# A first weight row loaded from two queues, and another number of unused products around the output projection

## The chip, the cores and the metric

The kernel runs on one core of a Trainium2 chip. The metric is the device time of one execution in microseconds (us), the median of several runs. A core has five engines that run at the same time: TensorE (PE in the profile, with its weight loads as PEld), VectorE (DVE), ScalarE (ACT), GpSimd (POOL) and SyncE (SP). SyncE computes nothing here, it issues the transfers. 16 DMA engines carry the transfers between memory and the core's buffers; SyncE and ScalarE each have a queue of their own from which these engines are fed.

## The reference

One decoding step of a transformer block for two sequences: a layer norm, attention over the last 2048 positions of a cache of 8192 (32 heads of 192), an output projection, and a gated feed-forward part, each with its residual.

```python
q = (x @ wq).reshape(B, Sq, Hq, Dh)            # B = 2, Sq = 1, D = 640, Hq = 32, Dh = 192
scores = einsum("bhqd,bhkd->bhqk", q, k) * Dh ** -0.5    # k, v: the last W = 2048 rows of the caches
o = einsum("bhqk,bhkd->bhqd", softmax(scores), v)
A = o.reshape(B, Sq, Hq * Dh) @ wo
h = x + A(layernorm(x))
out = h + (gelu(layernorm(h) @ w_gate) * (layernorm(h) @ w_up)) @ w_down     # F = 1536
```

All inputs are bfloat16. The kernel reads the windows of both caches and all weights once; it multiplies each of them with only two rows of x, h or the heads' results.

## The kernel before, in words

**How the work is written.** Each engine's program is a list of operations. `P.op` notes what an operation reads and writes (the names in `R`, `W` and `X`) and derives the semaphore waits between the engines from it; within an engine the order is that of the calls. An operation with `dma=` is a transfer, and each such name has a semaphore of its own. The helpers `pe`, `dve`, `act` and `pool` add an operation to their engine.

**How the work is staged.** A ring of three slots of 49152 bytes a partition takes everything large in turn: wq, eight loads each of K and V (6144 KB apiece), wo in two pieces (36 and 12 of its 48 rows a partition), then four of w_gate's five rows a partition, w_up in two pieces and w_down in four. `load` puts a transfer into a list, and `pump` issues from the head of the list on SyncE, as soon as all that lay in its place has been read (`done`). K is transposed on TensorE (L555), copied back by DVE and ScalarE, multiplied with q (L613), and the softmax of four groups at a time goes with V through TensorE (L669). The groups run in a loop of four trips on PE and DVE.

**The start.** x (`xrow`) is issued by ScalarE (L435). The first row a partition of w_gate does not go into the ring but into a buffer of its own, `wgh` (`load_wg0`, L397 to L399), issued by SyncE ahead of wq; it is read only by the first of the gate products near the end (L832). Then follow wq and the first loads of K (L372, the one line of all ring loads). x is turned into columns by PE (L496), normalised, and the products with wq (L575) wait for that and for wq's landing.

**The end.** After the loop, `spread(0)`, `behind(14)`, `heads_done(1)` and `spread(1)` gather the heads' results of both sequences into `ot`. `oproj(0)` and `oproj(1)` multiply `ot` with wo's two pieces (L727: 72 and 24 products of 320 columns, on four column strips of TensorE at once), beginning with two products that add x (L722). Then come the second normalisation (L735 to L821), the gate products with w_gate (L832), their columns through TensorE and the gelu on DVE and ScalarE (L841 to L869), the products with w_up (L832 again, into `ops`), their columns and the product with the gelu (`uT`), the products with w_down's four pieces (L881; the last piece has four products), a copy of the result (`yrow`, L887) and the store (L888).

**Unused products.** `keep_busy(n, w)` issues n products of the identity matrix with constants (`cf`) into a PSUM bank, whose result nobody reads. In 32-bit floats a product of 512 columns is two matmul rows of the profile (L752). They are placed in the loop's sums, behind q, and four times around the end: one product behind `behind(14)`, two behind `spread(1)`, and two between `oproj(0)` and `oproj(1)`.

Of the kernel before, what the change touches and what calls it, by code (L numbers as in the profile page):

```python
# [14 lines left out]
NC5 = D // 128  # L15
# [232 lines left out]
def bass_sequential_preLN__sliding_block_cached__geglu_ffn__decode_kernel(  # L248
# [12 lines left out]
    with ExitStack() as ctx:  # L261

        def sb(name, shape, dt):
            return ctx.enter_context(nc.sbuf_tensor(name, shape, dt))
# [31 lines left out]
        wgh = sb("wgh", [128, 1, F], BF16)  # L296
# [54 lines left out]
        P = _Prog()  # L351
        looped = []

        where, live, queue, used = {}, [], [], set()
# [33 lines left out]
        def load_wq():  # L388
            load("wq", WQ_AT, 2 * NC5 * HQ * DH, A_wq.rearrange("(p c) n -> p c n", c=NC5),
                 lambda v: v.rearrange("p (c n) -> p c n", n=HQ * DH), "wq")  # L390
# [4 lines left out]
                 lambda v: v.rearrange("p (kk n) -> p kk n", n=D), f"wo{i}")  # L395

        def load_wg0():  # L397
            where["wg", 0] = wgh[:, :, :], ["wgh"]
            P.op("sp", lambda e: e.dma_start(wgh[:, 0, :], B_w_gate.rearrange("(p c) f -> p c f", c=NC5)[:, 0, :]), W=["wgh"], dma="wg0")  # L399

        def load_ffn():
            load(("wg", 1), WG_AT, 2 * (NC5 - 1) * F, B_w_gate.rearrange("(p c) f -> p c f", c=NC5)[:, 1:NC5, :],
# [17 lines left out]
        def pe(fn, R=(), W=(), X=(), cls=0):  # L420
            return P.op("pe", fn, R, W, X, cls=cls)
# [10 lines left out]
        def tt(out, a, b, op):  # L432
            return lambda e: e.tensor_tensor(out=out, in0=a, in1=b, op=op)  # L433

        P.op("act", lambda e: e.dma_start(xrow[0:2, :], A_x[:, 0, :]), W=["xrow"], dma="dx")  # L435
        load_wg0()
        load_wq()
        for i in range(2 * NQ):
            load_k(i)
# [267 lines left out]
        def spread(b):  # L707
            pe(lambda e: e.matmul(sps[:, 0:DH], lhsT=colsel[:, :], rhs=onrm[:, b, :], start=True, stop=True), R=["colsel", ("onrm", b)], X=["s"])
            dve(tt(sm[:, 0:DH].rearrange("p (c k) -> p c k", c=4), sps[:, 0:DH].rearrange("p (c k) -> p c k", c=4),
                   oht[:, :].unsqueeze(2).to_broadcast([128, 4, 48]), ALU.mult), R=["oht"], W=["sm"], X=["s"])  # L710
            dve(lambda e: e.tensor_reduce(out=ot32[:, :], in_=sm[:, 0:DH].rearrange("p (c k) -> p k c", c=4), axis=AX.X, op=ALU.add),
                R=["sm"], W=["ot32"])
            dve(lambda e: e.tensor_copy(ot[:, :, b], ot32[:, :]), R=["ot32"], W=["ot"])

        def oproj(i):
            wo, wtoks = where["wo", i]
            k0, k1 = WOC[i]

            def fn(e):
                if i == 0:  # L720
                    for h in range(2):
                        e.matmul(m1[32 * h:32 * h + 2, 192:512], lhsT=identb[0:2, 0:2], rhs=xrow[0:2, 320 * h:320 * (h + 1)],  # L722
                                 start=True, stop=False, tile_position=(0, 32 * h), skip_group_check=True)
                for kk in range(k0, k1):
                    for h in range(2):
                        r = 2 * (kk % 2) + h
                        ins = e.matmul(m1[32 * r:32 * r + 2, 192:512], lhsT=ot[:, kk, :],  # L727
                                       rhs=wo[:, kk - k0, 320 * h:320 * (h + 1)], start=(kk == 1),
                                       stop=(kk >= 46), tile_position=(0, 32 * r), skip_group_check=True)
                return ins  # L730

            pe(fn, R=wtoks + ["ot", "xrow", "identb"], X=["m1"])
            done(("wo", i))
            if i == len(WOC) - 1:
                dve(lambda e: e.tensor_tensor_reduce(out=hrow[0:98, :], in0=m1[0:98, 192:512], in1=hrow[0:98, :], scale=1.0, scalar=0.0,  # L735
                                                     op0=ALU.add, op1=ALU.add, accum_out=rs[0:98, :]), R=["hrow"], W=["hrow", "rs"], X=["m1"])
# [12 lines left out]
        def keep_busy(n, w=4):  # L749
            def fn(e):  # L750
                for k in range(n):
                    ins = e.matmul(tps[3][:, 0:128 * w], lhsT=identf[:, :], rhs=cf[:, 0:w, :].rearrange("p k x -> p (k x)"), start=True, stop=True)  # L752
                return ins

            pe(fn, R=["identf", "cf0", "cfm"], X=[("t", 3)])
# [39 lines left out]
        keep_busy(1)  # L795
        heads_done(1)
        spread(1)
        keep_busy(2)
        for i in range(len(WOC)):
            oproj(i)  # L800
            if i == 0:
                keep_busy(2)

        pe(lambda e: e.matmul(tps[3][:, 0:2], lhsT=rs[0:98, :].to_broadcast([98, 128]), rhs=bsel[0:98, :], start=True, stop=True),
           R=["rs", "bsel"], X=[("t", 3)])
# [47 lines left out]
        def rjb(t):  # L853
# [18 lines left out]
            W=[("osb", 0), ("osb", 1)], X=["o"])  # L872
        vT = ffn_columns(urow, [("osb", 0), ("osb", 1)], tps[1], 1)
        dve(tt(uT[:, :, 0:17:16].rearrange("p (r j) b -> p r j b", r=4), vT, rjb(ga[:, 0, :]), ALU.mult), R=["ga0"], W=["uT"], X=[("t", 1)])
        for i, (f0, f1) in enumerate(WDC):
            wd, wtoks = where["wd", i]

            def fn(e, f0=f0, f1=f1, wd=wd):
# [10 lines left out]
             dma="dout")  # L889
# [43 lines left out]
```

## Time and profile before

| what | us |
|---|---|
| median of 3 runs | 291.8 (291.45 to 292.17) |
| the profiled execution | 291.8 |
| its span, first to last instruction | 290.5 |
| PE busy in the span | 192.6 (66%) |
| DVE busy | 144.2 (50%) |
| ACT busy | 94.8 (33%) |
| POOL busy | 17.4 (6%) |
| HBM read | 122.29 MB, 421 GB/s over the span |

The profile is one execution. Its page gives the busy time of each engine, the span in 40 slices, the DMA queues, the chain of work that ended last, the costliest groups of instructions and the DMA issues. A row of a group or of the timeline has the start and the duration in us, the engine, the line of the kernel, the operation, what it writes and reads, the shape and the number of instructions; in brackets stands the idle time of the engine ahead of it, with what ended it. In a table of stretches, each row has its bounds, its length, the busy time (and the instructions) of PE, PEld, DVE, ACT and POOL, the TensorE clock that was granted (1.00 is full speed), the mean share of the 16 DMA engines that was busy, and the GB/s that they moved. A DMA row gives the size of one issue and the time from its issue to its landing. Span and time differ by what lies around the first and the last instruction.

### The profile page before, as it was taken

The numbers are of one execution on the slowest core, as the hardware profiler recorded it, in microseconds if no ns is written. First come the engines' busy times: TensorE is split into PE (matmuls) and PEld (weight loads), VectorE is DVE, ScalarE is ACT, GpSimd is POOL, SyncE is SP. The second block draws the span as 40 slices with busy tenths as digits, with TensorE's granted clock in tenths as the row PEclk, the third lists the DMA queues.
The fourth block names the chain that finished last, engine by engine and source line by source line (L and its number), as shares of the span: only waits on it lengthen the run. The fifth ranks groups of instructions, "written<-read, shape, count | busy, mean of one in ns | idle before, by whom it ended". The sixth has DMA issues, their size and how long they took to land.

```text
span 290.5 us, 6244 instructions
## 1 busy us (share of the span) xinstructions
PE 192.6 (66%) x2587; PEld 149.2 (51%) x2587; DVE 144.2 (50%) x379; ACT 94.8 (33%) x128; POOL 17.4 (6%) x44
## 2 busy tenths in 40 slices
PE   1007378865962788688607886886078868879785
PEld 1004276654830677477206774772067747726443
DVE  6100036781474067757720777577206775776022
ACT  1001026652430067356100673561006735610001
POOL 7500200000020000000200000002000000000000
PEclk9999959999797599999975999999759999999785
DMA  8999999999999999999999999999999999999994
GB/s 325 415 492 440 423 435 433 429 433 429 433 429 433 433 433 433 428 433 433 433 433 433 433 433 433 433 433 433 433 433 433 433 433 433 423 419 395 412 413 160
DMA packets 3915, 122.45 MB, mean 422 GB/s; under 512 B 446, under 2 KB 576, under 8 KB 1216
## 3 DMA queue, kind: packets, MB, share of 16 engines
q1 hardware_dynamic: 3900, 122.29, 97.9%
q8 instruction: 8, 0.13, 0.2%
q14 instruction: 3, 0.02, 0.0%
q10 hardware_dynamic: 4, 0.00, 0.0%
HBM read 122.29 MB, written 0.00 MB: 421 GB/s over the span
## 4 chain that ended last, share of the span: by engine, by line
DMA 44%; PE 35%; issue 10%; DVE 8%; ACT 3%; SPq 0%; DVEq 0%
DMA ring<-in_A_v_cache_dram 24%; PE tpp L555 18%; DMA ring<-in_A_k_cache_dram 13%; DMA ring<-in_A_wo_dram 8%; PE ops L669 5%; PE m L669 4%; DVE eblk L657 2%; PE sps L613 2%; DVE ktr L566 2%; DVE et L653 2%; PE m L727 2%; ACT ktr L564 1%; ACT eexp L628 1%; PE tpp L752 1%; PE m L881 1%
## 5 line engine op out<-in xcount | busy, mean ns | idle before, releaser
L555 PE MATMUL tpp<-identf,ring 128*128 128x128 f32 x768 | 94.6, 283 | 19.3 <-DVE ktr L566 11.6
L564 ACT ACTIVATE ktr<-tpp 128x1024 bf16<-128x1024 bf16 x80 | 76.7, 1019 | 85.9 <-PE tpp L555 85.9
L555 PEld LDWEIGHTS tpp<-identf,ring 128*128 128x128 f32 x768 | 86.8, 145 | 28.0 <-DVE ktr L566 12.5
L566 DVE COPY ktr<-tpp 128x1024 bf16<-128x1024 bf16 x112 | 76.0, 690 | 39.9 <-PE tpp L555 38.2
L613 PE MATMUL sps<-ktr,rq 128*32 128x512 bf16 x384 | 24.8, 387 | 14.1 <-DVE ktr L566 14.1
L669 PE MATMUL ops<-ring,eblk 128*32 128x192 bf16 x512 | 15.9, 290 | 24.2 <-DMA ring<-in_A_v_cache_dram 24.2
L669 PEld LDWEIGHTS ops<-ring,eblk 128*32 128x32 bf16 x512 | 14.2, 121 | 25.5 <-DMA ring<-in_A_v_cache_dram 24.7
L628 ACT ACTIVATE eexp<-sm,nms 128x512 bf16<-128x512 f32 x16 | 11.6, 722 | 41.0 <-DVE nms L624 41.0
L613 PEld LDWEIGHTS sps<-ktr,rq 128*32 128x32 bf16 x384 | 9.9, 94 | 24.5 <-ACT ktr L564 17.8
L752 PE MATMUL tpp<-cf,identf 128*128 128x512 f32 (+1 forms) x62 | 22.5, 504 | 0.0
L657 DVE COPY eblk<-et 32x512 bf16<-32x512 bf16 x64 | 18.5, 289 | 1.8
L624 DVE CUSTOM_DVE_ANT_1 sm<-sps,mska 128x512 f32<-128x512 f32 x16 | 11.0, 687 | 16.4 <-issue 16.2
L433 POOL TENSOR_TENSOR rq<-qs,mask 128x192 bf16<-128x192 bf16 x16 | 7.8, 518 | 178.5 <-PE sps L613 162.0
L669 PE MATMUL m<-ring,eblk 128*32 128x192 bf16 x512 | 14.8, 275 | 2.8 <-issue 2.8
L669 PEld LDWEIGHTS m<-ring,eblk 128*32 128x32 bf16 x512 | 13.7, 119 | 3.0 <-issue 3.0
L575 PE MATMUL tpp<-ring,xnT 128*32 128x384 bf16 x80 | 5.1, 430 | 14.9 <-DMA ring<-in_A_wq_dram 14.9
L700 DVE SCALAR_TENSOR_TENSOR osum<-ops,wp,osum 128x192 f32<-128x192 f32 x4 | 1.7, 418 | 26.5 <-PE ops L669 26.4
L752 PEld LDWEIGHTS tpp<-cf,identf 128*128 128x128 f32 x62 | 10.0, 195 | 7.4 <-issue 7.3
L653 DVE STREAM_TRANSPOSE et<-eexp 128x512 bf16<-128x512 bf16 x16 | 11.3, 706 | 1.0
L575 PEld LDWEIGHTS tpp<-ring,xnT 128*32 128x32 bf16 x80 | 2.9, 125 | 16.7 <-issue 15.0
L598 DVE CAST qs<-ops 128x384 bf16<-128x384 f32 x1 | 0.6, 559 | 19.9 <-PE ops L593 19.9
L582 ACT ACTIVATE qrow<-tpp 128x768 bf16<-128x768 f32 x1 | 0.8, 811 | 19.4 <-PE tpp L575 19.4
(138 smaller groups left out, 84.8 us busy)
## 6 DMA issues: line engine op xcount, KB each, us to landing
ring<-in_A_k_cache_dram SPq DMA_DIRECT2D x8, 6144.0 KB, 29.0
ring<-in_A_v_cache_dram SPq DMA_DIRECT2D x8, 6144.0 KB, 24.1
ring<-in_A_wq_dram SPq DMA_DIRECT2D x1, 7680.0 KB, 21.1
ring<-in_A_wo_dram SPq DMA_DIRECT2D x1, 5760.0 KB, 22.5
ring<-in_A_wo_dram SPq DMA_DIRECT2D x1, 1920.0 KB, 21.5
ring<-in_B_w_gate_dram SPq DMA_DIRECT2D x1, 1536.0 KB, 24.8
ring<-in_B_w_up_dram SPq DMA_DIRECT2D x1, 1536.0 KB, 28.0
ring<-in_B_w_down_dram SPq DMA_DIRECT2D x1, 960.0 KB, 20.2
```

The lines of the kernel that those rows point to most:

```text
L433: return lambda e: e.tensor_tensor(out=out, in0=a, in1=b, op=op)
L555: ins = e.transpose(bank[:, 128 * u:128 * (u + 1)], kv[:, off:off + 128], identf[:, :])
L564: act(lambda e, dst=dst, src=src: e.activation(out=dst, in_=src, func=ACT.Copy), W=[("kt", n)], X=[x])
L566: dve(lambda e, dst=dst, src=src: e.tensor_copy(dst, src), W=[("kt", n)], X=[x], cls=0)
L575: ins = e.matmul(tps[0][32 * r:32 * (r + 1), 0:384], lhsT=xnT[:, c, 32 * J:32 * (J + 1)], rhs=wq[:, c, 1536 * J + 384 * r:1536 * J + 384 * ...
L613: ins = e.matmul(sps[32 * hg:32 * (hg + 1), :], lhsT=rq[:, k, hg, :], rhs=cols, start=(k == 0), stop=(k == 5), tile_position=(0, 32 * hg))
L624: dve(lambda e: e.tensor_tensor_reduce(out=sm[:, :].rearrange("p (u x) -> p u x", x=32), in0=sps[:, :].rearrange("p (u x) -> p u x", x=32) ...
L628: act(lambda e: e.activation(out=eexp[:, :], in_=sm[:, :], func=ACT.Exp, bias=nms[:, n:n + 1], scale=-1.0, accum_out=zr[:, n:n + 1]), R=[( ...
L653: dve(lambda e: e.transpose(et[:, :], eexp[:, :]), R=["eexp"] + [("eb", 0, 3)] * (g % 2), W=["et"], cls=0)
L657: dve(lambda e, hg=hg: e.tensor_copy(eblk[32 * hg:32 * (hg + 1), g % 2, :, hg, :], et[32 * hg:32 * (hg + 1), :].rearrange("p (a x) -> p a ...
L669: ins = e.matmul(bank[32 * r:32 * (r + 1), 0:DH], lhsT=eblk[:, g % 2, a, :, :].rearrange("p s x -> p (s x)")[:, r:128:4], rhs=vv[:, DH * t ...
L752: ins = e.matmul(tps[3][:, 0:128 * w], lhsT=identf[:, :], rhs=cf[:, 0:w, :].rearrange("p k x -> p (k x)"), start=True, stop=True)
```

## The change

The first row of w_gate is cut into two halves of 64 partitions. SyncE issues the lower one and ScalarE the upper one; each half has a semaphore and a token of its own, and the gate products wait for both. ScalarE issues its half ahead of x instead of x first. Behind `spread(1)` there are four unused products instead of two, and between `oproj(0)` and `oproj(1)` one instead of two.

```diff
         def load_wg0():
-            where["wg", 0] = wgh[:, :, :], ["wgh"]
-            P.op("sp", lambda e: e.dma_start(wgh[:, 0, :], B_w_gate.rearrange("(p c) f -> p c f", c=NC5)[:, 0, :]), W=["wgh"], dma="wg0")
+            where["wg", 0] = wgh[:, :, :], [("wgh", 0), ("wgh", 1)]
+            src = B_w_gate.rearrange("(p c) f -> p c f", c=NC5)
+            for k, eng in enumerate(("sp", "act")):
+                P.op(eng, lambda e, k=k: e.dma_start(wgh[64 * k:64 * (k + 1), 0, :], src[64 * k:64 * (k + 1), 0, :]), W=[("wgh", k)], dma=f"wg0{k}")
...
+        load_wg0()
         P.op("act", lambda e: e.dma_start(xrow[0:2, :], A_x[:, 0, :]), W=["xrow"], dma="dx")
-        load_wg0()
         load_wq()
...
         spread(1)
-        keep_busy(2)
+        keep_busy(4)
         for i in range(len(WOC)):
             oproj(i)
             if i == 0:
-                keep_busy(2)
+                keep_busy(1)
```

## The prediction

> **What bounds the kernel now.** I read the page first: the span, its slices and the DMA queues. The second line below is what the DMA engines moved in 40 slices of 7.26 us.
>
> ```profile
> span 290.5 us, 6244 instructions
> ...
> GB/s 325 415 492 440 423 435 433 429 433 429 433 429 433 433 433 433 428 433 433 433 433 433 433 433 433 433 433 433 433 433 433 433 433 433 423 419 395 412 413 160
> ...
> q1 hardware_dynamic: 3900, 122.29, 97.9%
> q8 instruction: 8, 0.13, 0.2%
> ```
>
> The 16 DMA engines move 433 GB/s in most slices, and little less in the others from the third to the last but one, and SyncE's queue alone fills 97.9% of their time. So the stream of loads is the bound: the end can come forward only if the stream starts sooner or if less is left to do after its last piece. I therefore went to both ends of the span, first the end. The DMA issues with their time to landing, and then SyncE's part of the timeline, give the moment at which each late weight is there (issue start plus landing time):
>
> ```profile
> ring<-in_A_wq_dram SPq DMA_DIRECT2D x1, 7680.0 KB, 21.1
> ring<-in_A_wo_dram SPq DMA_DIRECT2D x1, 5760.0 KB, 22.5
> ring<-in_A_wo_dram SPq DMA_DIRECT2D x1, 1920.0 KB, 21.5
> ring<-in_B_w_gate_dram SPq DMA_DIRECT2D x1, 1536.0 KB, 24.8
> ring<-in_B_w_up_dram SPq DMA_DIRECT2D x1, 1536.0 KB, 28.0
> ...
> wgh<-in_B_w_gate_dram SPq DMA_DIRECT2D x1, 384.0 KB, 3.3
> ring<-in_B_w_up_dram SPq DMA_DIRECT2D x1, 384.0 KB, 28.5
> ...
> ring<-in_B_w_down_dram SPq DMA_DIRECT2D x1, 160.0 KB, 21.3
> ```
> ```profile
> 247.59 0.34 SPq L372 DMA_DIRECT2D ring<-in_A_wo_dram  x1
> 253.08 0.33 SPq L372 DMA_DIRECT2D ring<-in_A_wo_dram  x1
> 253.46 0.43 SPq L372 DMA_DIRECT2D ring<-in_B_w_gate_dram  x1
> 253.94 0.91 SPq L372 DMA_DIRECT2D ring<-in_B_w_up_dram  x2
> ...
> 266.36 0.94 SPq L372 DMA_DIRECT2D ring<-in_B_w_down_dram  x1
> ```
>
> wo's first piece lands at 247.59 + 22.5 = 270.09, its second at 253.08 + 21.5 = 274.58, w_gate's four rows at 253.46 + 24.8 = 278.26, w_up's first piece at 253.94 + 28.0 = 281.94, its second at 282.92 (its issue starts 0.43, the time of the issue before it, ahead of 253.94 + 0.91 = 254.85, so at 254.42). The last piece of w_down lands at 266.36 + 21.3 = **287.66**. Now the timeline of the last 25 us, cut to the rows of the chain that ended last:
>
> ```profile
> 266.37 1.88 PE L752 MATMUL tpp<-cf,identf 128*128 128x512 f32 x4
> ...
> 270.19 0.30 PE L722 MATMUL m<-xrow,identb 2*2 2x320 bf16 x2 [1.93 <-DMA ring<-in_A_wo_dram]
> ...
> 270.41 3.98 PE L727 MATMUL m<-ring,ot 128*2 128x320 bf16 x72
> ...
> 274.32 2.25 PE L752 MATMUL tpp<-cf,identf 128*128 128x512 f32 x4
> ...
> 276.50 0.99 PE L727 MATMUL m<-ring,ot 128*2 128x320 bf16 x24
> ...
> 280.19 0.39 PE L832 MATMUL sps<-ring,hnT 128*2 128x384 bf16 x4
> ...
> 283.01 1.77 PE L832 MATMUL ops<-ring,hnT 128*2 128x384 bf16 x20
> ...
> 286.54 1.78 PE L881 MATMUL m<-ring,uT 128*17 128x160 bf16 x48 [0.32 <-DVE uT L433]
> 288.37 0.32 DVE L887 CAST yrow<-m 113x160 bf16<-113x160 f32 x1 [1.89 <-PE m L881]
> ```
>
> PE starts the first half of the output projection 0.10 after its load has landed (270.19 against 270.09), so I take 0.10 as the step from landing to PE. PE then has 1.93 us of idle time behind it. The clock, by stretches (the figure behind the five engines, then the DMA share and GB/s), shows what that does:
>
> ```profile
> 266.00:270.00 4.00, 2.25 (x7) 0.94 (x6) 1.03 (x3) 0.00 (x0) 0.00 (x0) 1.00 0.79 328
> ...
> 271.00:272.00 1.00, 1.00 (x28) 0.62 (x24) 0.00 (x0) 0.00 (x0) 0.00 (x0) 0.74 0.90 381
> ...
> 274.00:275.00 1.00, 1.00 (x9) 0.50 (x2) 0.00 (x0) 0.00 (x0) 0.00 (x0) 0.55 1.01 418
> ...
> 282.00:283.00 1.00, 0.68 (x3) 0.46 (x3) 0.27 (x1) 0.00 (x0) 0.00 (x0) 0.50 0.99 407
> ```
>
> A stretch at 0.74 is half of it at 1.00 and half at 0.50, one at 0.55 a tenth of it at 1.00: the granted clock falls to 0.50 at about 271.5 and comes back near 274.9; the 72 products of wo's first piece, and part of the unused products behind them, run at half speed. Near 282 it falls again for the rest.
>
> **The change, part by part.** *Four unused products instead of two behind the last spread.* One `keep_busy` product is two rows of the profile: the four rows at 266.37 take 1.88, 0.47 each. Eight rows take 3.76 and end at 270.13, before PE can start at 270.19: cost nothing, hidden by the wait for wo's first piece. If that load came sooner, they would cost up to their excess, and PE has room for that (below). The gap in PE's work is closed, so I expect the clock to hold at 1.00 through wo's first piece. At full clock 24 products take 0.99, so 72 take at most 2.97: from 270.41 to 273.4 instead of 274.4.
>
> *One unused product instead of two between wo's pieces.* At full clock 2 rows, 0.94 us: to 274.3. What is late next is the load: wo's second piece can start at 274.58 + 0.10 = 274.68. PE ends it at 275.67 instead of 277.49: **1.8 us gained on PE**.
>
> *Where that gain goes.* I carry it along the chain. w_gate's ring rows: 280.19 - 1.8 = 278.39, and they have landed (278.36 with the step): the gain stays 1.8. The w_up products: 283.01 - 1.8 = 281.2, but the load allows 282.04: the gain shrinks to 0.97. At the half clock of before, 20 products take 1.77, so they end at 283.81, after w_up's last piece (283.02). So uT is ready 0.97 sooner and the w_down products may start at 286.54 - 0.97 = 285.57. But their last piece is not there before 287.66 + 0.10 = 287.76, and behind it come four products. One of them takes 338 ns by the row below; four overlapping ones take 0.34 to 0.44 (1.78 - 0.34 = 1.44 over the other 47, 0.03 each).
>
> ```profile
> L881 PE MATMUL m<-ring,uT x48: 303/338/341, 286.5 to 288.0; 128*17 128x160 bf16 x48
> ```
>
> So the copy of y starts between 288.12 and 288.22, 0.15 to 0.25 sooner than at 288.37. I take **-0.2**. Of 1.8 us gained on PE, 1.6 are taken back by the landing of the last 160 KB. The same sum says how much PE may be late without harm: about 1.6 us at the projection. So a product too many, or a clock that falls in another place, costs nothing at the end either.
>
> *w_gate's first row in two halves.* At the start of the span:
>
> ```profile
> 0.72 0.54 ACTq L435 DMA_DIRECT2D xrow<-in_A_x_dram  x1
> 0.72 0.38 SPq L399 DMA_DIRECT2D wgh<-in_B_w_gate_dram  x1
> ...
> 1.17 0.41 SPq L372 DMA_DIRECT2D ring<-in_A_wq_dram  x1
> ```
> ```profile
> PE tpp L575 <- DMA ring<-in_A_wq_dram: 14.9, 1, 14.9
> ACT lt L487 <- PE m L485: 5.0, 1, 5.0
> ```
>
> ScalarE now issues its half at 0.72 and x behind it, 0.38 to 0.54 later; its table load moves by the same, under 5.0 us of idle time. If x also lands behind a half of w_gate it is some 4 us late or less (3.3 is the landing of the whole row). PE, and DVE with it, would start the first normalisation that much later; PE has 14.9 us of waiting for wq behind that normalisation: cost nothing. The halves themselves are not read before 280. What counts is whether wq's load begins sooner, since all later loads queue behind it. The issue on SyncE stays one instruction (0.33 to 0.43 in the rows above for loads from 384 to 7680 KB, and 0.94 only for the last), so wq's issue hardly moves; the bytes and the 16 engines are the same. Bounds: at best the half that leaves SyncE's queue goes wholly beside other start-up time, 192 KB at 433 GB/s = -0.45; at worst SyncE's issue takes ScalarE's 0.54 instead of 0.38, +0.16. No row lies nearer to one end: I take a value near the middle, **-0.1**.
>
> The Trainium skill, page "DMA: Bandwidth & Descriptors", section "Rules for kernel authors", speaks against this edit: two transfers to disjoint partition halves are not worth it, since both use the same 16 engines. By that rule this term is 0 and the sum 291.6; no row of this trace shows two halves side by side.
>
> **Sum.** The profiled execution took 291.8 us, of which the span is 290.5, and 291.8 is also the median of the three runs. 291.8 - 0.2 - 0.1 = **291.5 us**. About 0.3% (0.88 us) is what a measurement of this kernel can tell from no change, so this counts as no change.
>
> **The rivals.** *The clock falls anyway.* The Trainium skill, page "TensorE: Matmul & The Clock Gate", section "Why this matters for your kernels", warns of PE gaps above about 3 us; here the clock fell after a gap of 1.93, so the gap may not be its cause. As a mechanism of this kernel: wo's first piece still ends at 274.4, one product fewer takes 0.94 off, the second piece starts at 275.6, and PE is 0.9 sooner; w_down's products could run from 285.6 to 287.4 and still wait for 287.76: 291.5 to 291.6. Against it: from 266 to 270 the clock is still 1.00, behind PE work with no such gap, and it returned to 1.00 once PE had worked on without one. Chance 0.10, counted as no change.
>
> *The whole PE gain arrives.* 291.8 - 1.8 = 290.0, if the last landing did not bind. The row of 21.3 us speaks against it, and the change moves no w_down issue. Chance 0.02.
>
> *The start gives much more.* wq lands at 1.17 + 21.1 = 22.27; it and w_gate's row are 8064 KB, 8.26 MB, 19.1 us at 433 GB/s; before 1.50 no engine moves data:
>
> ```profile
> 0.00:1.50 1.50, 0.00 (x0) 0.00 (x0) 0.69 (x13) 0.21 (x1) 0.87 (x8) 1.00 0.00 0
> ```
>
> So 22.27 - 1.50 - 19.1 = 1.7 us are lost to slow first packets and to landing. If two queues at once fill the engines sooner and recover half of it, the stream is 0.85 earlier and the time 291.8 - 0.2 - 0.85 = 290.75. For it: the row lands only after 3.3 us although 384 KB are 0.9 us of transfer. Against it: nothing shows that a second queue shortens a first packet. Chance 0.12.
>
> *Slower: an instruction packet on an engine that ends last.* Some DMA engines end about 1.5 us before others:
>
> ```profile
> 285.75:286.25 0.50, 0.47 (x3) 0.17 (x2) 0.00 (x0) 0.00 (x0) 0.00 (x0) 0.50 0.56 220
> ...
> 286.75:287.25 0.50, 0.50 (x24) 0.50 (x20) 0.00 (x0) 0.00 (x0) 0.00 (x0) 0.50 0.21 74
> ```
>
> A share of 0.56 is 9 of 16 engines still at work. The 8 packets of the instruction queue take 0.2% of 16 x 290.5 us, about 1.2 us each on one engine, near that difference. The change makes PE's program longer by one product and moves PE's code in time; if one more such packet falls on one of the nine late engines, the last piece lands 1.2 to 1.5 us later. At 1.5 the time is 291.5 + 1.5 = 293.0. It decides from a second packet on one engine; below that the seven early engines absorb it. Against it: eight packets so far, and the late engines look as if each was hit once. Chance 0.08.
>
> **Chances and range.** My forecast keeps 0.68. Faster: 0.12 + 0.02, and 0.02 for the forecast's own lower end, 0.16. Slower: 0.08, and 0.02 for its upper end, 0.10. Within 0.3%: 0.74. The forecast's bounds are 291.8 - 0.25 - 0.45 = 291.1 and 291.8 - 0.15 + 0.16 = 291.8; the runs before spread from 291.45 to 292.17, about 0.35 to each side of their median. That gives 290.8 to 292.2, which leaves out the slower rival, the whole PE gain and about half of the start's.
>
> **What would show it.** Right: eight rows of unused products ending near 270.1; the clock 1.00 from 266 to 274; the second piece of wo starting near 274.7; idle time of PE before the last w_down products, released by their DMA; the copy of y starting 0.4 to 0.6 after that landing. Wrong: w_down's last landing moved against the output's end by more than 0.2, or wq's landing moved from 22.27 by more than 0.4; or a last landing that falls a microsecond behind the others. If the last products do not wait for a DMA, my main step has failed.

## The result, and the profile after

The changed kernel takes **293.65 us** (median of 18 runs) against 291.8 us before (median of 18 runs): a ratio of 1.0052, 95% interval 1.0041 to 1.0063. By the medians it is 1.85 us slower; the ratio, which is not that of the medians, makes it 1.5 (1.2 to 1.8). Three executions in the experiments, of 314.99, 488.52 and 1018.21 us, lie far outside all others: the ratios leave them out, and they move no median given here by more than 0.06. The runs of the changed kernel fall into two groups, 7 of 18 at 292.3 to 292.9 (median 292.35, 0.55 above before) and 11 of 18 at 293.5 to 294.3 (median 293.81, 2.01 above). The profiled execution, 292.33 us, is one of the lower group, so it can show only the loss that every run has; an execution of the upper group was caught in an experiment (e15). In the changed kernel the lines behind the edit stand two further down (L752 is L754, L881 is L883).

The page of the changed kernel, beside the same lines of before in the prediction:

```profile
span 291.0 us, 6249 instructions
...
GB/s 325 405 405 432 429 428 432 428 432 435 426 428 432 439 432 432 434 432 439 432 432 432 432 432 432 439 432 439 439 439 432 439 432 432 431 450 389 405 416 174
...
q1 hardware_dynamic: 3836, 122.10, 97.7%
q10 hardware_dynamic: 84, 0.20, 0.2%
q8 instruction: 8, 0.13, 0.2%
```

The stream is as dense as before. SyncE's queue has 64 packets fewer (3836 for 3900), ScalarE's (q10) has 84 where it had 4, and the instruction queue still has its 8 packets. What differs at the start is slice 3, 405 GB/s where it was 492, and at the end the last slice, 174 where it was 160: the same bytes arrive later. The first transfers of the timeline and the times to landing of the changed kernel show where that begins:

```profile
0.72 0.59 SPq L401 DMA_DIRECT2D wgh<-in_B_w_gate_dram  x1
0.73 0.56 ACTq L401 DMA_DIRECT2D wgh<-in_B_w_gate_dram  x1
...
1.33 0.76 ACTq L438 DMA_DIRECT2D xrow<-in_A_x_dram  x1
1.37 0.83 SPq L372 DMA_DIRECT2D ring<-in_A_wq_dram  x1
```
```profile
ring<-in_A_wq_dram SPq DMA_DIRECT2D x1, 7680.0 KB, 21.6
...
wgh<-in_B_w_gate_dram SPq DMA_DIRECT2D x1, 192.0 KB, 4.2
wgh<-in_B_w_gate_dram ACTq DMA_DIRECT2D x1, 192.0 KB, 3.2
ring<-in_B_w_down_dram SPq DMA_DIRECT2D x1, 160.0 KB, 19.2
```

Half the row takes SyncE longer to issue than the whole row did (0.59 against 0.38), and wq's issue behind it takes 0.83 against 0.41. So wq's issue ends at 1.37 + 0.83 = 2.20, before at 1.17 + 0.41 = 1.58. wq lands at 1.37 + 21.6 = 22.97 against 22.27, **0.70 later**. (The page rounds a time to landing to 0.1; the landings in the trace itself are 22.24 and 23.01, which makes it 0.77.) In the packets of the trace, wq's first packet begins on the 16 engines at 3.3 to 3.9, before at 2.9 to 3.7, and takes 2.6 to 3.1, before 2.3 to 2.5. The first data of all come later too. The stretches of the changed kernel, then that of before (the last two figures are the DMA share and GB/s):

```profile
1.50:2.00 0.50, 0.00 (x0) 0.00 (x0) 0.48 (x3) 0.00 (x0) 0.50 (x1) 1.00 0.00 0
2.00:2.50 0.50, 0.00 (x0) 0.00 (x0) 0.39 (x2) 0.37 (x1) 0.50 (x1) 1.00 0.75 160
```
```profile
1.50:2.00 0.50, 0.00 (x0) 0.00 (x0) 0.48 (x3) 0.50 (x1) 0.50 (x1) 1.00 0.79 91
```

Between 1.50 and 2.00 the engines were already 79% busy before; now nothing moves before 2.00. At the other end, the issue of w_down's last piece in SyncE's part of the timeline, and then the timeline of PE and DVE, both of the changed kernel:

```profile
269.32 0.96 SPq L372 DMA_DIRECT2D ring<-in_B_w_down_dram  x1
```
```profile
269.33 3.60 PE L754 MATMUL tpp<-cf,identf 128*128 128x512 f32 x8
...
272.86 0.29 PE L724 MATMUL m<-xrow,identb 2*2 2x320 bf16 x2
...
273.08 2.62 PE L729 MATMUL m<-ring,ot 128*2 128x320 bf16 x72
...
275.63 1.13 PE L754 MATMUL tpp<-cf,identf 128*128 128x512 f32 x2
...
276.68 0.99 PE L729 MATMUL m<-ring,ot 128*2 128x320 bf16 x24
...
287.08 1.78 PE L883 MATMUL m<-ring,uT 128*17 128x160 bf16 x48 [0.31 <-DVE uT L435]
288.91 0.33 DVE L889 CAST yrow<-m 113x160 bf16<-113x160 f32 x1 [1.89 <-PE m L883]
```

The last piece of w_down lands at 269.32 + 19.2 = 288.52 (before 287.66: **+0.86**), and y is copied at 288.91, 0.39 behind that landing (before 288.37 - 287.66 = 0.71: **-0.32**). Together +0.54; the two profiled executions differ by 292.33 - 291.8 = 0.53. So this execution is explained by its two ends: the stream 0.86 later, less left to do behind it. PE itself came late here (eight unused rows at 269.33, not near 266.4), probably because the clock was at half in a further stretch of the loop (from 239 to 244 us the granted clock was 0.66 on the mean, before 1.00). Its last products follow `uT` (0.31) and not a DMA, so this profile does not have the wait for w_down that the prediction named as a sign of being right. The profiles of e2, e14 and e15 have it (0.18, 0.21 and 0.22).

### The profile page after: what moved, and what is told of

The parts are those of the page before. It is cut to its first block, busy times and chain, and to the rows that moved or that the text cites. A ratio compares the mean times of both kernels' runs of the same rounds, so it can differ in the third digit from the quotient of the medians.

```text
span 291.0 us, 6249 instructions
## 1 busy us (share of the span) xinstructions
PE 197.4 (68%) x2589; PEld 153.2 (53%) x2589; DVE 144.5 (50%) x379; ACT 95.3 (33%) x128; POOL 17.4 (6%) x44
## 3 DMA queue, kind: packets, MB, share of 16 engines
q1 hardware_dynamic: 3836, 122.10, 97.7%
## 4 chain that ended last, share of the span: by engine, by line
PE 41%; DMA 36%; issue 10%; DVE 9%; ACT 3%; SPq 0%; DVEq 0%
DMA ring<-in_A_v_cache_dram 23%; PE tpp L557 22%; DMA ring<-in_A_k_cache_dram 13%; PE ops L671 5%; PE m L671 5%; DVE eblk L659 3%; DVE et L655 2%; DVE ktr L568 2%; PE sps L615 2%; PE tpp L754 2%; ACT ktr L566 1%; PE m L729 1%; ACT eexp L630 1%; PE m L883 1%; PE ops L834 1%
## 5 line engine op out<-in xcount | busy, mean ns | idle before, releaser
L557 PE MATMUL tpp<-identf,ring 128*128 128x128 f32 x768 | 98.5, 291 | 18.7 <-DVE ktr L568 11.6
L557 PEld LDWEIGHTS tpp<-identf,ring 128*128 128x128 f32 x768 | 91.1, 150 | 27.5 <-DVE ktr L568 12.5
L671 PEld LDWEIGHTS ops<-ring,eblk 128*32 128x32 bf16 x512 | 13.9, 121 | 24.5 <-DMA ring<-in_A_v_cache_dram 23.2
L754 PE MATMUL tpp<-cf,identf 128*128 128x512 f32 (+1 forms) x64 | 23.0, 503 | 0.0
L577 PE MATMUL tpp<-ring,xnT 128*32 128x384 bf16 x80 | 5.9, 484 | 15.5 <-DMA ring<-in_A_wq_dram 15.5
L671 PE MATMUL m<-ring,eblk 128*32 128x192 bf16 x512 | 14.9, 276 | 1.7 <-issue 1.7
L754 PEld LDWEIGHTS tpp<-cf,identf 128*128 128x128 f32 x64 | 10.2, 191 | 7.6 <-issue 7.5
## 6 DMA issues: line engine op xcount, KB each, us to landing
ring<-in_A_wq_dram SPq DMA_DIRECT2D x1, 7680.0 KB, 21.6
ring<-in_B_w_gate_dram SPq DMA_DIRECT2D x1, 1536.0 KB, 22.7
```

Source lines behind the costliest of these rows:

```text
L557: ins = e.transpose(bank[:, 128 * u:128 * (u + 1)], kv[:, off:off + 128], identf[:, :])
L577: ins = e.matmul(tps[0][32 * r:32 * (r + 1), 0:384], lhsT=xnT[:, c, 32 * J:32 * (J + 1)], rhs=wq[:, c, 1536 * J + 384 * r:1536 * J + 384 * ...
L671: ins = e.matmul(bank[32 * r:32 * (r + 1), 0:DH], lhsT=eblk[:, g % 2, a, :, :].rearrange("p s x -> p (s x)")[:, r:128:4], rhs=vv[:, DH * t ...
```

## The experiments

Each ratio is that of the kernel to the one before on the same chip, with its 95% interval, and behind it the medians in us. The theories carry letters in what was expected. For e1 to e4: by A both edits cost something, by B the start does all, by C the products do all.

**e1: the row's halves alone**, as in the change, with the products of before. Edit to the changed kernel:

```diff
-        keep_busy(4)
+        keep_busy(2)
...
-                keep_busy(1)
+                keep_busy(2)
```

> Only the split of w_gate's first row and the new order on ScalarE; the unused products stay at two and two. Theory A (two causes): the two queues issue at once, each issue takes longer (0.59 and 0.83 us on SyncE instead of 0.38 and 0.41), wq lands about 0.8 us later (near 23.0 instead of 22.24), and the whole stream with it: 0.4 to 0.8 us slower than before, 292.2 to 292.6, with the spread of before and no second group of runs. Rival B (the start does all): the median lies near that of the whole change, 293.3 to 293.9, with runs in two groups 1.4 us apart. Rival C (the products do all): within 0.2 us of before.

1.0033 (1.0017 to 1.0049), 292.39 against 291.56: **+0.83**. 8 of 11 runs are below 292.7, 3 are at 293.3 to 294.0. SyncE's issues took 0.60 and 0.82. The halves alone bring a loss, and already both groups of times. Its size is near the one that A gave, the two groups are those of B. The interval overlaps that of the whole change (1.0041 to 1.0063), so no difference between the two is shown.

**e2, e3, e4: the products alone**, the row whole and on SyncE as before. Edit of e2 to the kernel before; e3 has the second half of it alone (two and one), e4 the first alone (four and two):

```diff
-        keep_busy(2)
+        keep_busy(4)
...
-                keep_busy(2)
+                keep_busy(1)
```

> Only the numbers of unused products (four and one); w_gate's first row is loaded as before. Theory A: PE is late at the end in part of the executions, because the clock falls during the last groups; there two more products (four rows of 0.47 us, or twice that at half clock) delay wo's first products. Median 0.3 to 1.3 us above before, with runs in two groups. Rival B: within 0.2 us of before. Rival C: 1.5 to 2 us above.

> Two products behind the last spread as before, one instead of two between wo's pieces. Theory A: one product less can only help where PE is late: 0 to 0.8 us faster than before, median near 291.5. Rivals B and C: within 0.2 us of before.

> Four products behind the last spread, two between wo's pieces as before. Theory A: the cost of the two added products without the one that is saved: 0.5 to 0.9 us above the run with four and one. Rival B: within 0.2 us of before. Rival C: the products behind the spread cost 1.5 us or more.

e2 0.9997 (0.9986 to 1.0007), 291.58 against 291.56; e3 0.9999 (0.999 to 1.0008), 291.56; e4 1.0002 (0.9993 to 1.0011), 291.57. The products do nothing that can be measured: C falls, and A as far as it gave them a cost; of the three, B is left, with a smaller size than it gave. The timeline of e2 shows why:

```profile
266.25 3.60 PE L752 MATMUL tpp<-cf,identf 128*128 128x512 f32 x8
...
270.31 0.29 PE L722 MATMUL m<-xrow,identb 2*2 2x320 bf16 x2 [0.46 <-DMA ring<-in_A_wo_dram]
...
270.53 2.62 PE L727 MATMUL m<-ring,ot 128*2 128x320 bf16 x72
...
274.76 0.99 PE L727 MATMUL m<-ring,ot 128*2 128x320 bf16 x24 [0.56 <-DMA ring<-in_A_wo_dram]
...
287.40 0.72 PE L881 MATMUL m<-ring,uT 128*17 128x160 bf16 x12 [0.18 <-DMA ring<-in_B_w_down_dram]
...
288.17 0.32 DVE L887 CAST yrow<-m 113x160 bf16<-113x160 f32 x1 [2.51 <-PE m L881]
```

The eight rows end at 269.85, before wo is there; the 72 products take 2.62 in place of 3.98; wo's second piece starts at 274.76 in place of 276.50. And then the last products wait for w_down: PE's 1.7 us end in front of a load.

**e5: the changed kernel again**, without an edit, on another chip.

> The changed kernel again, beside its variants and for a second profile. The split alone was 0.33% slower than before, the products alone 0.03% faster: if the two add up, the whole change is 0.7 to 0.9 us slower than before on this chip, with some runs 1.2 to 1.8 us above that. If the products make the split worse (PE later at the end by more rows that nobody needs), the median is 1.5 us or more above before.

1.0047 (1.0033 to 1.0062), 292.87 against 291.59: +1.28, runs from 292.18 to 294.3. The loss is there on this chip too, and its runs are as wide. But three of the ten lie at 293.0 to 293.2, between the two groups: here the groups are not parted. 1.28 also lies between the two sizes expected and decides neither.

From here on all kernels have the products of before (two and two), if nothing else is said, and the edit shown is the one to the rest of the changed kernel. In e6 to e8, A is that two queues prolong each other's issues, B that the cut into halves costs, whichever engine issues them.

**e6: both halves on SyncE.**

```diff
-            for k, eng in enumerate(("sp", "act")):
+            for k, eng in enumerate(("sp", "sp")):
```

> Split as in the change, but SyncE issues both halves one behind the other, x alone on ScalarE; unused products as before. Theory A (two queues that issue at the same time prolong each other's issues, and wq's descriptors come late): SyncE's issues take about 0.4 us each, the engines are busy with the halves until 3.5 us anyway, wq lands within 0.25 us of 22.24: within 0.3 us of before. Rival B (the cut into halves costs, whoever issues them): as slow as the split alone, 0.7 to 0.9 us above before.

1.007 (1.0054 to 1.0085), 293.85 against 291.59: +2.26. In the timeline of e6:

```profile
0.72 1.22 SPq L401 DMA_DIRECT2D wgh<-in_B_w_gate_dram  x2
1.98 0.59 SPq L372 DMA_DIRECT2D ring<-in_A_wq_dram  x1
```

Each half takes 0.61 and wq's issue 0.59, with no second queue at work on the row. A falls as the main cause: the half is slow to issue by itself. The size that B gave, 0.7 to 0.9, is missed as well: wq is issued 0.81 later than before and lands at 1.98 + 21.8 = 23.78.

**e7: x behind ScalarE's table load**, to keep x's issue away from wq's.

```diff
         load_wg0()
-        P.op("act", lambda e: e.dma_start(xrow[0:2, :], A_x[:, 0, :]), W=["xrow"], dma="dx")
...
         act(lambda e: e.preload_act_table_set("natural_log_exp_and_others"))
+        P.op("act", lambda e: e.dma_start(xrow[0:2, :], A_x[:, 0, :]), W=["xrow"], dma="dx")
```

> The split with ScalarE's half at once, but x issued behind ScalarE's table load, so that wq's issue on SyncE has no other issue beside it. Theory A: SyncE's first issue still takes 0.59, wq's takes 0.41 instead of 0.83, wq's first packets take 2.27 us instead of 2.7 to 3.1: 0.2 to 0.5 us above before. Rival B, or a cost of the two queues in the DMA engines themselves: still 0.7 to 0.9 us above before.

1.0077 (1.0064 to 1.0091), 294.07 against 291.59. The timeline of e7:

```profile
1.36 0.73 ACTq L474 DMA_DIRECT2D xrow<-in_A_x_dram  x1
1.37 0.82 SPq L372 DMA_DIRECT2D ring<-in_A_wq_dram  x1
```

x is still issued at 1.36, beside wq: the table load did not hold it back. The edit did not do what it was made for, and this run decides nothing between A and B. Its first issues on SyncE are those of e1 (0.59, then 0.82), yet three of its runs lie at 294.0 to 294.1: how many runs fall into the upper group is not settled by these issues.

**e8: x first on ScalarE**, its half of the row behind it.

```diff
-        load_wg0()
         P.op("act", lambda e: e.dma_start(xrow[0:2, :], A_x[:, 0, :]), W=["xrow"], dma="dx")
+        load_wg0()
```

> The split with ScalarE's order of before: x first, then its half. Theory A: SyncE's half is issued beside x, wq beside ScalarE's half, so wq's issue is still prolonged: 0.3 to 0.9 us above before. If the order on ScalarE is what costs, within 0.2 us of before.

1.0036 (1.0023 to 1.005), 292.41 against 291.59: +0.82. SyncE's rows of e8:

```profile
0.72 0.59 SPq L401 DMA_DIRECT2D wgh<-in_B_w_gate_dram  x1
1.37 0.57 SPq L372 DMA_DIRECT2D ring<-in_A_wq_dram  x1
```
```profile
ring<-in_A_wq_dram SPq DMA_DIRECT2D x1, 7680.0 KB, 21.6
```

wq's issue now takes 0.57 and not 0.83, with ScalarE's half beside it in place of x. (x's issue beside it does not prolong it in every case: in e9 x is issued at 1.15, and wq's issue takes 0.41.) But wq lands at 1.37 + 21.6 = 22.97, as in the changed kernel, and the loss is no smaller than in e1: the 0.26 more that wq's own issue took there is not the price. What is left is the half's 0.59, by which wq's issue begins 0.20 later, and what comes behind it. The next two theories: D, a transfer over 64 partitions is what costs; E, two transfers in place of one.

**e9: halves by columns.** Both halves reach over all 128 partitions and take 768 of the 1536 columns each, on the same two queues.

```diff
-                P.op(eng, lambda e, k=k: e.dma_start(wgh[64 * k:64 * (k + 1), 0, :], src[64 * k:64 * (k + 1), 0, :]), W=[("wgh", k)], dma=f"wg0{k}")
+                P.op(eng, lambda e, k=k: e.dma_start(wgh[:, 0, 768 * k:768 * (k + 1)], src[:, 0, 768 * k:768 * (k + 1)]), W=[("wgh", k)], dma=f"wg0{k}")
```

> The row is cut by columns, not by partitions: two transfers of 128 partitions and 768 columns, SyncE the first, ScalarE the second ahead of x; unused products as before. Theory D (a transfer over 64 partitions takes longer to issue, 0.6 instead of 0.38 us, and delays the first bytes from 1.73 to 2.08): the issues are back at about 0.4, first bytes at 1.73: within 0.3 us of before. Rival E (two transfers in place of one at the start cost, whatever their shape): 0.7 us or more above before.

1.0003 (0.9994 to 1.0011), 291.59 against 291.73: **the loss is gone**. The first issues of e9, and its first data:

```profile
0.72 0.40 ACTq L401 DMA_DIRECT2D wgh<-in_B_w_gate_dram  x1
0.72 0.39 SPq L401 DMA_DIRECT2D wgh<-in_B_w_gate_dram  x1
...
1.17 0.41 SPq L372 DMA_DIRECT2D ring<-in_A_wq_dram  x1
```
```profile
1.50:2.00 0.50, 0.00 (x0) 0.00 (x0) 0.48 (x3) 0.27 (x1) 0.50 (x1) 1.00 0.46 80
```

The same bytes, queues and number of transfers, only another shape: issues of 0.39 to 0.41, wq at 1.17 as before, data before 2.00. E falls, D stands. With the shape goes the number of packets, though: in the trace a half by columns is 128 packets of 1.5 KB, a half by partitions 64 of 3 KB. No run separates the two.

**e10: the whole row on ScalarE**, ahead of x; SyncE begins with wq.

```diff
-            for k, eng in enumerate(("sp", "act")):
-                P.op(eng, ...)
+            P.op("act", lambda e: e.dma_start(wgh[:, 0, :], B_w_gate.rearrange("(p c) f -> p c f", c=NC5)[:, 0, :]), W=["wgh"], dma="wg0")
```

> The whole row on ScalarE ahead of x, SyncE begins with wq at 0.72. Theory D: all transfers are of 128 partitions, wq's issue comes 0.45 us sooner: 0 to 0.4 us faster than before. Theory A (issues of two queues at the same time prolong each other): wq's issue takes about 0.8, its first packets 2.7 or more: 0.2 to 0.8 us slower. Rival E: within 0.2 us of before.

1.0106 (1.009 to 1.0122), 294.45 against 291.73: +2.72, outside all three expectations. The timeline of e10:

```profile
0.72 0.40 ACTq L399 DMA_DIRECT2D wgh<-in_B_w_gate_dram  x1
...
1.16 0.55 ACTq L436 DMA_DIRECT2D xrow<-in_A_x_dram  x1
...
1.17 34.99 SPq L372 DMA_DIRECT2D ring<-in_A_k_cache_dram  x2
...
25.88 0.33 PE L496 MATMUL m<-identb,xrow 2*128 2x2 bf16 x5 [25.88 <-DMA xrow<-in_A_x_dram]
```

x was issued at 1.16 behind the row and was there only at 25.88, when wq had landed too (22.7). q and with it the release of wq's place in the ring came late: the second K load's issue ended at 1.17 + 34.99 = 36.16, before at 28.07, and the stream has a hole: from 38 to 39 us the share of busy DMA engines is 0.11. By the packets of the trace the 16 engines lose about 0.8 us around it; where the rest of the loss comes from is not shown.

**e11: the row whole, on SyncE behind wq and the first K.** Edit to the kernel before:

```diff
-        load_wg0()
         load_wq()
...
         pump()
+        load_wg0()
```

> The whole row on SyncE, behind wq and the first K load: the stream begins with wq's large packets at 0.72. If the small first packets cost time at the start (128 packets took 22 engine-us, 1.4 us an engine, for 0.9 us of bytes): 0.3 to 0.5 us faster than before. If the first bytes cost the same whichever transfer comes first: within 0.2 us.

1.0025 (1.0014 to 1.0036), 292.47 against 291.73: +0.74, although wq is issued 0.45 sooner; neither expectation held:

```profile
0.72 0.39 SPq L372 DMA_DIRECT2D ring<-in_A_wq_dram  x1
...
1.85 0.90 SPq L399 DMA_DIRECT2D wgh<-in_B_w_gate_dram  x1
```

By the trace wq lands 0.48 sooner, but its first packets take 2.3 to 3.7 us each, most of them 2.27 before: it looks as if a slow start is paid by whatever comes first, and the row had paid it. Between the K loads the row seems to cost more than that: by the trace the last landing of w_down is at 288.51 in place of 287.63.

**e12: the lower half at the start, the upper half behind the first K**, both on SyncE, x alone on ScalarE.

```diff
-        def load_wg0():
+        def load_wg0(k):
...
-            for k, eng in enumerate(("sp", "act")):
-                P.op(eng, ...)
+            P.op("sp", lambda e: e.dma_start(wgh[64 * k:64 * (k + 1), 0, :], src[64 * k:64 * (k + 1), 0, :]), W=[("wgh", k)], dma=f"wg0{k}")
...
-        load_wg0()
+        load_wg0(0)
...
         pump()
+        load_wg0(1)
```

> The lower half on SyncE at the start, the upper half on SyncE behind the first K load, x alone on ScalarE: one transfer of 64 partitions ahead of wq and no second one. Theory D: the issue takes 0.6, first bytes at 2.08, wq later than it could be: 0 to 0.5 us slower than before although half of the row's bytes are gone from the start. Rival E: the second transfer is gone, wq comes sooner: 0.2 to 0.4 us faster than before.

1.008 (1.0066 to 1.0093), 294.02 against 291.73: +2.29, all five runs at 293.7 to 294.1. SyncE's rows of e12:

```profile
0.72 0.59 SPq L400 DMA_DIRECT2D wgh<-in_B_w_gate_dram  x1
1.37 0.57 SPq L372 DMA_DIRECT2D ring<-in_A_wq_dram  x1
...
2.63 1.01 SPq L400 DMA_DIRECT2D wgh<-in_B_w_gate_dram  x1
```

A single transfer over 64 partitions ahead of wq gives the issues of e8, with nothing of the row on ScalarE: two queues are not needed for them. D had the issue right (0.6) and the size wrong (0 to 0.5). wq's first packets begin at 2.8 to 4.3, most of them no later than before, but take 2.5 to 3.5. The rest of the loss is put down to the later half, as it was to the row in e11, but no run shows that half alone: behind it the 16 parts of each K or V load land over 2.8 us, in place of 2.1 before.

**e13: the whole change, with halves by columns** (the edit of e9, products four and one).

> The whole change (four and one unused products, two queues, ScalarE's half ahead of x) with the row cut by columns instead of partitions. Theory D (only the 64 partitions of a half cost): within 0.2 us of before, no runs above 292.6. If the products and the split make each other worse: 0.5 us or more above before.

0.9997 (0.9987 to 1.0008), 291.61 against 291.62, all 12 runs between 291.4 and 292.1. With the shape alone altered, the whole loss of the change is gone, the upper group too. wq is issued at 1.17 and lands at 22.2 (in e9 at 22.5).

**e14, e15, e16: the changed kernel, one profile each**, for one of the upper group. F: a DMA engine that is late already is held up once more. G: PE is late.

> The changed kernel once more, for one profile. If its time is 293.5 us or more: theory F (one DMA engine that began late is held up again by a packet of instructions): w_down's last piece lands 1 us or more later than the 288.48 of the profile shown, and the last of the 16 landings of a K or V load comes 2.6 us or more behind the first. Rival G (PE late): that landing stays near 288.5, and the copy of y starts more than 0.6 us behind it. If the time is near 292.3, it repeats the profile shown.

> As the look before this one: theory F or rival G where its time is 293.5 us or more, by w_down's last landing against 288.48; else a repetition of the profile shown.

> As the two looks before this one: theory F or rival G where its time is 293.5 us or more, by w_down's last landing against 288.48; else a repetition of the profile shown.

292.3, 294.02 and 292.63 us. e14 repeats the profile above, with w_down's last landing at 288.4; e15 is of the upper group. Its landings and the issue of w_down's last piece, then its last rows of PE and DVE, and the stretches at its end:

```profile
ring<-in_A_wq_dram SPq DMA_DIRECT2D x1, 7680.0 KB, 23.3
...
ring<-in_B_w_down_dram SPq DMA_DIRECT2D x1, 160.0 KB, 19.6
```
```profile
270.51 0.43 SPq L372 DMA_DIRECT2D ring<-in_B_w_down_dram  x1
```
```profile
289.80 0.71 PE L883 MATMUL m<-ring,uT 128*17 128x160 bf16 x12 [0.22 <-DMA ring<-in_B_w_down_dram]
...
290.56 0.33 DVE L889 CAST yrow<-m 113x160 bf16<-113x160 f32 x1 [2.56 <-PE m L883]
```
```profile
288.00:289.00 1.00, 0.94 (x24) 0.65 (x24) 0.01 (x1) 0.00 (x0) 0.00 (x0) 0.50 0.14 56
289.00:290.00 1.00, 0.78 (x24) 0.37 (x20) 0.00 (x0) 0.00 (x0) 0.00 (x0) 0.50 0.05 18
```

w_down's last piece lands at 270.51 + 19.6 = 290.11, 2.45 later than before, and PE waits for it: G falls. From 289 to 290 us a share of 0.05, less than one engine of 16, is still at work. wq's landing is at 24.7. In the trace the first packet of wq begins at 4.6 to 5.5 on four engines (2.9 to 3.7 on all of them before), and the 16 parts of a K or V load land over 2.9 us from the first load on and over 3.5 from the fifth on: both signs of F, and as if the engines that began late stay behind (the trace does not say which engine a packet is on). In e16 two engines begin as late (5.0 and 5.2) and wq lands at 24.5, but the parts land within 2.2 and the time is 292.63; the profile of e7 is like it (4.8 and 5.1, 24.6, within 2.1, 292.44). So a late start of single engines is there in the one profile of the upper group, and is not enough for it; whether it is needed is not shown. That an instruction packet then falls on one of them is only argued.

## Why the prediction was wrong

**What bounds the kernel: right.** The end lies 0.39 behind w_down's last landing in the changed kernel, 0.41 in e2 and 0.45 in e15, and PE's gain at the projection was taken back there, as worked out: in e2 w_up's products start behind their load at 282.18 (forecast 282.04) and w_down's at 285.71 (forecast 285.57). The sign "idle time of PE before the last w_down products" is in e2, e14 and e15, and not in the first profile of the changed kernel, where PE was late.

**The products: right in mechanism, too small to measure.** In e2 the four products hide under the wait for wo, the clock is 1.00 from 266 to 277 (it falls at 278, where before it fell at 271.5 and again near 282), the second piece of wo starts at 274.76 (e2; forecast 274.68), and the copy of y stands at 288.17 (forecast 288.12 to 288.22; its own terms, 287.76 and 0.34 to 0.44, give 288.10 to 288.20). The -0.2 is that of the profiled executions (291.59 in e2 against 291.8), and single runs of one kernel differ by more; of the medians it is +0.02, and the interval of the ratio (-0.41 to +0.20) holds both. The rival in which the clock falls anyway, and the one in which all of PE's gain arrives, did not occur: 72 products took 2.62, and 1.7 us on PE brought nothing that can be measured.

**x behind a half: right.** PE's wait for wq behind the first normalisation is still there, 15.5 us where it was 14.9 (the group of the products with wq on the page of the changed kernel):

```profile
L577 PE MATMUL tpp<-ring,xnT 128*32 128x384 bf16 x80 | 5.9, 484 | 15.5 <-DMA ring<-in_A_wq_dram 15.5
```

It would have been wrong for a whole row ahead of x (e10).

**The start: the step that failed**, word for word "The issue on SyncE stays one instruction [...] so wq's issue hardly moves". It took the issue's duration from the rows of wq, wo and the later weights and counted instructions, not shapes. SyncE's timeline of before had a row that could have warned, a K load, whose source has the 32 heads outermost:

```profile
54.36 0.54 SPq L372 DMA_DIRECT2D ring<-in_A_k_cache_dram  x1
```

And the 0.54 of x, which is two rows, was read as ScalarE's; that engine issues the whole row in 0.40 (e10). On SyncE the half over 64 partitions takes 0.59, and wq's issue behind it 0.57 to 0.83. In the changed kernel wq's issue thus began 0.20 and ended 0.62 later, and wq landed 0.70 later. The upper bound of +0.16 had the row's own issue at 0.54, in which it was close; it left out what comes behind it, wq's issue and its slower first packets. How the 0.70 is shared between these is not shown: in e8 wq's issue ends 0.26 sooner, and wq lands no sooner. One sign of being wrong came with it: wq's landing moved by more than 0.4. (The other, w_down's landing moved against the end by more than 0.2, came too, 0.71 to 0.39; but the prediction's own end, 0.4 to 0.6 behind that landing, asks for such a move, so it says nothing against it.) Measured alone the term is **+0.83** (e1), not -0.1; in the change, with more of its runs in the upper group, +1.85. By the ratios these are 0.96 and 1.52, with intervals that overlap.

The rule of the Trainium skill, page "DMA: Bandwidth & Descriptors", section "Rules for kernel authors", that two transfers to disjoint partition halves are not worth it, is borne out by e1 (1.0033). The 0 that the prediction made of it is nearer than -0.1, but short of +0.83. By columns the term is 0 (e9: 1.0003).

**The slower rival** named the right place, an engine that ends last, and nearly the right price: 1.2 to 1.5 us, where the upper group's median lies 1.46 above the lower's. But its trigger was PE's longer program, and the instruction queue has 8 packets as before; e2 has that program and no upper group, e1 has the upper group without it. That the price fits is luck as far as the runs show. What the upper group follows is the 64-partition shape (e13 has none of it), and in e15 a late start of some engines.

**Still open:** why a 64-partition transfer is slower to issue and to begin, whether its partitions or its packets make the difference, what holds up the late engine a second time, and what sets how many runs fall into the upper group. No version tried is measurably faster than the kernel before.

## What to carry to other kernels

A transfer is not priced by bytes and count alone: look in the trace for one of the same shape before you call its issue free, above all at the head of a stream that bounds the kernel, where a delay can go through to the end (here 0.70 at wq and 0.86 at w_down's last piece). If a load there must be cut, try columns first and keep all partitions in each part: here that cost nothing. Before PE time is bought, find the landing that the end waits for: 1.7 us won in front of it came to nothing.

## What the runs showed of the hardware

**Issue time goes with the shape.** With 128 partitions an issue took 0.38 to 0.41 at the start, for 192 KB (e9) as for 384 and 7680 KB (before); with 64 partitions 0.52 to 0.61 for 192 KB. The number of partitions is not all of it: the K loads fill 128 partitions from a source with 32 heads outermost and took 0.54 (before), and the row over 128 partitions took 0.90 behind wq and a K load (e11).

**A small transfer can wait for a large one on another queue.** x is two rows of 640 values; issued at 1.16 on ScalarE behind a whole row, it was there at 25.88, behind wq on SyncE (e10). In the changed kernel, issued at 1.33 and so 0.04 ahead of wq, it does no harm.

**A spread between the DMA engines lasts.** The time over which the 16 parts of a load land is nearly the same from the fifth K or V load to the last: 2.0 in e13, 2.1 before, 2.5 in e11, 2.7 in e6, 2.8 in e12, 3.5 in e15. The two profiles near 294.0 us are those with 2.8 and 3.5, and their last piece of w_down lands at 290.2 and 290.1. The spread alone does not give the time: e10 has 2.1 and lands at 289.7.
